# Linear attention and an ELU feed-forward on one core: mm1 in units of two chunks, state decay on GpSimd, two chunks transposed by DMA, one load on a second queue, in a new order of work

## The chip, the cores and the metric

One core of one Trainium2 chip. The metric is the device time of one execution in microseconds (us), the median of several. All runs quoted here are in the fast state with a granted TensorE clock of 0.99 to 1.00. "Span" is the profiled part of an execution; in most runs the time is 1.7 to 1.9 us above it, in a few up to 2.8 (the profiled run of split: 223.31 against 220.5).

## The reference

Two steps. A chunked linear attention with one decay factor per head, then a two-layer feed-forward with ELU between:

```python
# q, k, v: (4, 8, 768, 64); lam: (8,); w_in: (512, 2048); w_out: (2048, 512); all float32
for b in range(nb):                                   # blocks of the sequence
    intra = (qb @ kb^T) * Dmask ; intra = intra @ vb  # Dmask: lam ** (i - j), causal
    inter = (qb * lam_pow) @ kv_state
    out   = intra + inter
    kv_state = lam_block * kv_state + (kb * rev_pow)^T @ vb
x = attention as (3072, 512)
h = x @ w_in
g = where(h > 0, h, exp(min(h, 0)) - 1)               # ELU
return g @ w_out
```

(Shortened; einsums written as products.)

## The kernel before

The kernel works in 24 chunks of 128 rows (4 batches of 6), in a hand-written order of tokens. For a chunk g: `T` transposes q and k, `S` makes the scores psS, `E` masks them into pp, `P` makes the attention output psO and copies it into xt, `U` updates the state. `1:g:j` is one mm1 unit: 16 matmuls of xt with `w_in` into a psH bank (one of two), then e = exp on ScalarE, relu on ScalarE in place, and later g = min(e - 1, relu) on VectorE, which frees the bank. `2:g:j` is one mm2 unit: 4 matmuls of g with `w_out` into psM. Each engine executes its own instructions in the order in which they are written. The parts that the change touches:

```python
GPE = 10                       # chunks below GPE are transposed by PE, the others by DMA
POOL_ORDER = ("iota q1 k1 v1 v0 i1 i0 k2 q2 v2 o0 o1 i3 i2 q3 i5 k3 o2 d0 o3 i4 v3 ...")
OPEN = ("... P4 U4 2:3:2 1:4:0 P5 U2 1:4:1 V3 2:3:3 T6 U5 1:4:2 2:4:0 1:4:3 T7 2:4:1 U3 "
        "1:5:0 1:5:1 2:4:2 S6:7 1:5:2 2:5:0 2:4:3 P6 1:5:3 E7 T8 T9 ... S8:9 2:6:0 E9")
LAGU, LAG_END = 3, 4           # mm2 follows mm1 at 3 units, 4 at the end
# [...]
def att_U(g):
    # [4 matmuls into pu]
    for hh in range(2):
        r = slice(hh * 64, (hh + 1) * 64)
        # [first chunk of a batch: copy]
        (nc.gpsimd if g >= GPE else nc.vector).tensor_tensor(      # stt: decay of the old state
            out=tmp[r], in0=old[r, :, r],
            in1=upp[r].unsqueeze(2).broadcast_to([64, NHP, 64]), op=ALU.mult)
        nc.vector.tensor_tensor(out=new[r, :, r], in0=tmp[r], in1=pu[r, :, r], op=ALU.add)  # st
# [...]
def mm1(g, j):
    flush()                                                        # emits the g that is pending
    # [...]
    pH = ps.tile([128, FB, 128], FP32, tag="psH", bufs=2, name=f"psH{g}_{j}")
    for f in range(FB):
        i, w = wi_of[j * FB + f]
        for kk in range(NHP):
            nc.tensor.matmul(
                pH[:, f, :], lhsT=wi16[i][:, kk, w * 128 : (w + 1) * 128],
                rhs=xt[g][:, kk, :], start=(kk == 0), stop=(kk == NHP - 1))
    e = msb.tile([128, FB, 128], FP32, tag="e", bufs=3, name=f"e{g}_{j}")
    nc.scalar.activation(e[:], pH[:], AF.Exp)
    nc.scalar.activation(pH[:], pH[:], AF.Relu)
    pending.append(((g, j), e, pH))
```

`POOL_ORDER` is the order on GpSimd: loads of q, k, v, of `w_in` blocks (i) and `w_out` blocks (o), and d, the product kd of k with its decay.

Of the kernel before, what the change touches and what calls it, by code (L numbers as in the profile page):

```python
# [7 lines left out]
FP32 = mybir.dt.float32  # L8
# [7 lines left out]
def kernel(  # L16
# [20 lines left out]
    NG = B * NCB  # L37
    FB = 4
    NJ = NFT // FB
    GPE = 10  # L40
    WI = [2] * 8
    WO = [2] * 8
    POOL_ORDER = (
        "iota q1 k1 v1 v0 i1 i0 k2 q2 v2 o0 o1 i3 i2 q3 i5 k3 o2 d0 o3 i4 v3 o5 o4 d2 o7 i6 d3 "
        "d1 i7 o6 q4 k4 v4 q6 d4 k8 k6 v6 d5 d6 k10 q8 d7 q10 v8 v10"
    )
    RAW = "q0 k0"
    FIRST = "q0:0 c0 k0:1 c1 c2"
    OPEN = (
        "V0 Z1 z1 V1 z0 v3:1 Z0 z3 z2 T0 T1 S0 S1 P0 P1 1:0:0 T2 1:1:0 S2 2:0:0 Z2 P2 1:2:0 "  # L50
        "1:0:1 2:1:0 1:1:1 U0 T3 2:2:0 1:2:1 S3 2:0:1 2:1:1 1:0:2 1:1:2 P3 2:2:1 1:2:2 2:1:2 "
        "1:3:0 Z3 U1 2:0:2 1:3:1 1:0:3 2:2:2 1:1:3 2:0:3 1:2:3 T5 2:1:3 1:3:3 T4 2:2:3 1:3:2 "
        "S4:5 2:3:0 E5 2:3:1 P4 U4 2:3:2 1:4:0 P5 U2 1:4:1 V3 2:3:3 T6 U5 1:4:2 2:4:0 1:4:3 T7 "
        "2:4:1 U3 1:5:0 1:5:1 2:4:2 S6:7 1:5:2 2:5:0 2:4:3 P6 1:5:3 E7 T8 T9 1:6:2 V2 P7 U6 "
        "2:5:1 U7 1:6:0 2:5:2 2:5:3 1:6:1 S8:9 2:6:0 E9"
    )
    LAGU, LAG_END = 3, 4
    AT = {"W": -13, "T": -9, "S": -8, "P": -5, "U": -3}
    TAGS = {
        "S0": "M0 M1", "S1": "C D", "S2": "A B", "S3": "A B",  # L60
# [13 lines left out]
    ps = ctx.enter_context(tc.tile_pool(name="ps", bufs=1, space=bass.MemoryType.PSUM))  # L74

    lam_b = cpool.tile([128, H], FP32, name="lam_b")
    nc.scalar.dma_start(out=lam_b[:], in_=lam.unsqueeze(0).broadcast_to([128, H]))
    nc.scalar.preload_act_table_set("natural_log_exp_and_others")



# [12 lines left out]
    def emit_load(w, g0):  # L94
        n = size_of[g0]
        c, b = divmod(g0, B)
        x = {"q": q, "k": k, "v": v}[w]
        src = x[b : b + n, :, c * L : (c + 1) * L].rearrange("b h p d -> p (b h) d")
        if w == "v":
            t = vz1[g0] if n == 1 else vz2[(g0 - 4) // 2 % PB]  # L100
            vg[g0] = t
            dst = t[:, :, 0::2, :]
        else:
            t = asb.tile([128, n, H, 64], FP16, tag=f"{w}n{n}", name=f"{w}n{g0}", bufs=4)
            (qg if w == "q" else kg)[g0] = t
            dst = t[:]
        nc.gpsimd.dma_start(out=dst.rearrange("p b h d -> p (b h) d"), in_=src)  # L107
# [3 lines left out]
    for w in RAW.split():  # L111
        x = {"q": q, "k": k}[w[0]]
        g0 = int(w[1:])
        raw[w] = asb.tile([128, H, 64], FP32, name=f"raw_{w}", tag=f"raw_{w}")
        nc.sync.dma_start(out=raw[w][:], in_=x[g0, :, 0:L].rearrange("h p d -> p h d"))

    def cast_raw(g, w, eng):
        n = f"{w}{g}"
# [40 lines left out]
        nc.gpsimd.iota(iota_c[:], pattern=[[0, 1]], base=0, channel_multiplier=1)  # L159
        nc.gpsimd.iota(iota_r[:], pattern=[[1, 128]], base=0, channel_multiplier=0)  # L160

    kds, qkT, Pt, psS, psO, xt = {}, {}, {}, {}, {}, {}

    def att_kd(g):
        if g // B == NCB - 1:
# [11 lines left out]
    def emit_pool():  # L177
        w = pool_list.pop(0)
        if w == "iota":
            emit_iota()  # L180
        elif w[0] in "qkv":
            emit_load(w[0], int(w[1:]))
        else:
            {"i": emit_wi, "o": emit_wo, "d": att_kd}[w[0]](int(w[1:]))

    while pool_list and pool_list[0][0] != "d":
        emit_pool()

    def zero_v1(i, eng=0):
# [124 lines left out]
    def att_P(g):  # L314
        cb, b = divmod(g, B)
        vt = of(vg, g)
        qt, _ = qkT[g]
        po = bank(f"P{g}", 0, [128, NHP, 128], FP32, f"psO{g}")
        for hp in range(NHP):
            for hh in range(2):  # L320
                b0 = 4 * hp + hh
                nc.tensor.matmul(  # L322
                    po[:, hp, :], lhsT=vt[:, b0 : b0 + 2, :], rhs=Pt[(g, hh)][:, hp, :],
                    start=(hh == 0), stop=(hh == 1 and cb == 0), skip_group_check=True,
                )
            if cb > 0:
                nc.tensor.matmul(  # L327
                    po[:, hp, :], lhsT=st[b][cb % 2][:, hp, :], rhs=qt[:, hp, :],
                    start=False, stop=True, skip_group_check=True,
                )  # L330
        xt[g] = asb.tile([128, NHP, 128], FP16, tag="xt", name=f"xt{g}", bufs=6)
        if g < GPE:
            nc.scalar.copy(out=xt[g][:], in_=po[:])  # L333
        else:
            nc.vector.tensor_tensor(out=xt[g][:], in0=po[:], in1=qs[:], op=ALU.mult)  # L335

    def att_U(g):
        cb, b = divmod(g, B)
        if cb == NCB - 1:
            return  # L340
        vt = of(vg, g)
        pu = bank(f"U{g}", 0, [128, NHP, 128], FP32, f"psU{g}")
        for hp in range(NHP):
            nc.tensor.matmul(  # L344
                pu[:, hp, :].rearrange("p (h e) -> p h e", h=2),
                lhsT=kds[g][:, 2 * hp : 2 * hp + 2, :],
                rhs=vt[:, 4 * hp : 4 * hp + 3 : 2, :], start=True, stop=True,
            )
        new, old = st[b][(cb + 1) % 2], st[b][cb % 2]
        for hh in range(2):  # L350
            r = slice(hh * 64, (hh + 1) * 64)
            if cb == 0:
                nc.vector.tensor_copy(new[r, :, r], pu[r, :, r])
            else:
                tmp = asb.tile([128, NHP, 64], FP32, tag="stt", name=f"stt{g}_{hh}", bufs=4)
                (nc.gpsimd if g >= GPE else nc.vector).tensor_tensor(  # L356
                    out=tmp[r], in0=old[r, :, r],
                    in1=upp[r].unsqueeze(2).broadcast_to([64, NHP, 64]), op=ALU.mult,
                )
                nc.vector.tensor_tensor(  # L360
                    out=new[r, :, r], in0=tmp[r], in1=pu[r, :, r], op=ALU.add
                )


    gts, psM, stores, pending = {}, {}, [], []
# [5 lines left out]

    def flush():
        while pending:
            u, e, r = pending.pop(0)
            g = msb.tile([128, FB, 128], FP16, tag="g", bufs=24, name=f"g{u[0]}_{u[1]}")
            nc.vector.scalar_tensor_tensor(  # L376
                out=g[:], in0=e[:], scalar=-1.0, in1=r[:], op0=ALU.add, op1=ALU.min
            )
            gts[u] = g

    def mm1(g, j):
        flush()
        emit_stores(1)
        pH = ps.tile([128, FB, 128], FP32, tag="psH", bufs=2, name=f"psH{g}_{j}")
        for f in range(FB):
            i, w = wi_of[j * FB + f]
            for kk in range(NHP):
                nc.tensor.matmul(  # L388
                    pH[:, f, :], lhsT=wi16[i][:, kk, w * 128 : (w + 1) * 128],
                    rhs=xt[g][:, kk, :], start=(kk == 0), stop=(kk == NHP - 1),  # L390
                )
        e = msb.tile([128, FB, 128], FP32, tag="e", bufs=3, name=f"e{g}_{j}")
        nc.scalar.activation(e[:], pH[:], AF.Exp)  # L393
        nc.scalar.activation(pH[:], pH[:], AF.Relu)  # L394
        pending.append(((g, j), e, pH))

    mm2_done = {g: 0 for g in range(NG)}

    def mm2(g, j, last=False):
# [6 lines left out]
        for hi, cols in enumerate(halves):  # L406
            for f in range(FB):
                i, w = wo_of[j * FB + f]
                nc.tensor.matmul(  # L409
                    psM[g][:, cols], lhsT=gts[(g, j)][:, f, :], rhs=wo16[i][:, w, cols],  # L410
                    start=first and f == 0, stop=end and f == FB - 1, skip_group_check=True,
                )
            if end:
                out_of(g, cols, nc.vector if last and hi == 0 else nc.scalar)
# [18 lines left out]
    def pool_work(g):  # L433
        if group_of[g][1] == 0 and g + 4 < NG:
            for w in "qkv":
                emit_load(w, g + 4)
        att_kd(g)
        if g >= GPE:
            att_T_dma(g)

# [1 line left out]

    def ready(t):

        if t[0] in "12":
            return
        g = int(t[1:].split(":")[0])
        if t[0] == "P":
# [9 lines left out]
    def run(t):  # L458
# [10 lines left out]
        else:  # L469
            {"T": att_T_pe, "E": att_E, "P": att_P, "U": att_U, "1": mm1, "2": mm2,  # L470
             "V": zero_v, "Z": zero_st, "v": zero_v1, "z": zero_st1,
             "q": lambda g, e: cast_raw(g, "q", e), "k": lambda g, e: cast_raw(g, "k", e),
             "c": lambda i: (emit_qs, emit_mask, emit_ks)[i](), "W": pool_work, "O": emit_stores}[t[0]](*a)

    for t in FIRST.split():
        run(t)
    while pool_list:
        emit_pool()

    prog = OPEN.split()  # L480
    done = set(prog)
    m1 = [(g, j) for g in range(NG) for j in range(NJ) if f"1:{g}:{j}" not in done]
    m2 = [(g, j) for g in range(NG) for j in range(NJ) if f"2:{g}:{j}" not in done]
    extra = {}
    for g in range(0, NG, 2):
        u = 4 * g
        for t, p in (
            (f"W{g}", AT["W"]), (f"W{g + 1}", AT["W"] + 2),
            (f"T{g}", AT["T"]), (f"T{g + 1}", AT["T"] + 1),
# [7 lines left out]
            if t in done or f"{t[0]}{h}" in done or t[0] == "E" and f"S{h}" in done:  # L497
                continue
            extra.setdefault(u + p, []).append(t)
    first = 4 * NG - len(m1)  # L500
    for p in sorted(extra):
        if p < first:
            prog += extra.pop(p)
    n2 = 4 * NG - len(m2)
    for x, (g, j) in enumerate(m1):
        u = first + x
        prog.append(f"1:{g}:{j}")
        prog += extra.pop(u, [])
        lag = LAG_END if u >= 4 * NG - 8 else LAGU
        n = 0  # L510
        while m2 and n2 <= u - lag and n < 2:
            prog.append("2:%d:%d" % m2.pop(0))
            n2 += 1
            n += 1
    for g, j in m2:
        prog.append(f"2:{g}:{j}")
    prog[-1] += ":1"
# [33 lines left out]
```

## Time and profile before

| | before |
|---|---|
| time | 222.81 us median of 4 (222.52 to 223.24) |
| span of the profiled run | 221.4 us |
| PE matmuls | 2548 |
| bare matmul time (worked out below) | 198.8 us |
| PE without matmul issue | 22.6 us |

One more view is needed later: the groups on VectorE by shape from 48 to 87 us, with busy time, mean ns and then the idle time just before the group.

```profile
L376 DVE SCALAR_TENSOR_TENSOR g<-e,psH 128x512 f16<-128x512 f32 x17 | 11.6, 685 | 2.9 <-ACT psH L394 2.1 <-PE psS L300 0.5
L356 DVE TENSOR_TENSOR stt<-st,upp 64x256 f32<-64x256 f16 x12 | 8.0, 666 | 0.1
```

In these 39 us VectorE has 2.9 us of slack ahead of its 17 g, and the decays stt take 8.0 us of it. A g that comes late is one that PE waits for.

For PE I also use a sum of my own over the trace's matmul starts: each matmul is given its undisturbed step (55.6 ns for 128 columns, 108.9 for 256, 215.7 for 512, 34.5 for psS), and what a start is later than that is a gap. "Gap" means this everywhere below. Such a gap includes the drain of a wait, so it is larger than the "idle before" that the profile prints.

### The profile page before, as it was taken

Reading aid. Unit: us, or ns where it says so; the run is one execution under the profiler, and the core shown is the slowest. Engines: PE = TensorE matmul, PEld = TensorE weight load, DVE = VectorE, ACT = ScalarE, POOL = GpSimd, SP = SyncE. Lnnn points to the kernel's source line nnn. Section 1 sums busy time; section 2 is a strip of 40 time slices with the busy share of each in tenths; the row PEclk is TensorE's granted clock in tenths of the full one; section 3 lists DMA queues with packets and bytes.
Section 4 is the critical chain, followed back from the end, with each engine's and each line's share of the span. In section 5 each row is a group of like instructions: output and inputs, shape, how many; then the busy total and the mean of one; then the engine's idle time right before and its main releaser. Section 6 shows DMA issues by size and latency. Waiting matters only on the chain.

```text
span 221.4 us, 6086 instructions
## 1 busy us (share of the span) xinstructions
PE 207.1 (94%) x2548; PEld 156.3 (71%) x2548; DVE 138.6 (63%) x238; ACT 134.8 (61%) x255; POOL 88.6 (40%) x102
## 2 busy tenths in 40 slices
PE   0598999999999999999999999999999999999993
PEld 0486677768768776787787787787787777777761
DVE  5744745489978978666666666656657646634330
ACT  5745657766768566636636636646646645656760
POOL 8996990829972809508508508122000000000000
PEclk9999999999999999999999999999999999999999
DMA  7999999999999999968998998803304401101102
GB/s 114 169 182 186 195 200 167 139 169 120 166 140 181 127 164 135 141 84 93 143 100 100 132 108 95 144 0 98 94 3 98 96 3 47 52 1 50 47 3 95
DMA packets 99804, 24.26 MB, mean 110 GB/s; under 512 B 90432, under 2 KB 96832, under 8 KB 99776
## 3 DMA queue, kind: packets, MB, share of 16 engines
q0 software_dynamic: 78720, 13.37, 83.8%
q1 hardware_dynamic: 20912, 10.49, 22.3%
q8 instruction: 20, 0.33, 0.6%
q14 instruction: 8, 0.07, 0.1%
q10 hardware_dynamic: 144, 0.00, 0.0%
HBM read 27.27 MB, written 6.29 MB: 152 GB/s over the span
## 4 chain that ended last, share of the span: by engine, by line
PE 79%; DVE 11%; ACT 5%; DMA 2%; issue 1%; SPq 0%; DVEq 0%; ACTq 0%
PE psH L388 34%; PE psM L409 33%; PE psO L322 5%; DVE g L376 3%; PE psS L300 3%; DVE stt L356 2%; DMA raw_k<-in_k_dram 2%; PE psO L327 2%; DVE pp L309 2%; PE psU L344 2%; DVE qT L288 1%; DVE st L360 1%; ACT e L393 1%; ACT psH L394 1%; PE psT L281 1%
## 5 line engine op out<-in xcount | busy, mean ns | idle before, releaser
L388 PEld LDWEIGHTS <-wi 128*128 128x128 f16 x1536 | 94.0, 98 | 22.0 <-issue 2.2
L388 PE MATMUL psH<-xt,wi 128*128 128x128 f16 x1536 | 102.2, 220 | 1.8 <-ACT xt L333 0.7
L393 ACT ACTIVATE e<-psH 128x512 f32<-128x512 f32 x96 | 57.3, 597 | 68.3 <-PE psH L388 68.0
L409 PE MATMUL psM<-wo,g 128*128 128x512 f16 (+1 forms) x388 | 97.6, 377 | 0.8 <-DVE osb L422 0.5
L376 DVE SCALAR_TENSOR_TENSOR g<-e,psH 128x512 f16<-128x512 f32 x96 | 65.6, 684 | 44.1 <-ACT psH L394 42.8
L394 ACT ACTIVATE psH<-psH 128x512 f32<-128x512 f32 x96 | 56.9, 593 | 0.0
L409 PEld LDWEIGHTS <-g 128*128 128x128 f16 x388 | 33.7, 98 | 26.8 <-issue 0.7
L309 DVE TENSOR_TENSOR pp<-psS,mask 128x512 f16<-128x512 f32 x48 | 30.7, 682 | 5.1 <-PE psS L300 5.1
L107 POOL DMA_DIRECT2D vz<-in_v_dram x14 | 15.1, 1085 | 38.5 <-PE psU L344 38.0
L169 POOL TENSOR_TENSOR kd<-kn,ks 128x512 f16<-128x512 f16 x20 | 21.3, 1073 | 11.2 <-DMA kn<-in_k_dram 10.6
L322 PE MATMUL psO<-pp,vz 128*128 128x128 f16 x192 | 19.1, 226 | 1.2 <-DVE pp L309 1.2
L360 DVE TENSOR_TENSOR st<-stt,psU 64x256 f16<-64x256 f32 x32 | 13.4, 419 | 7.3 <-PE psU L344 6.3
L335 DVE TENSOR_TENSOR xt<-psO,qs 128x512 f16<-128x512 f32 x14 | 9.7, 691 | 11.9 <-PE psO L327 11.9
L322 PEld LDWEIGHTS <-vz 128*128 128x128 f16 x192 | 15.1, 101 | 2.5 <-issue 1.8
L424 ACT COPY osb<-psM 128x512 f32<-128x512 f32 (+1 forms) x24 | 13.9, 579 | 4.5 <-PE psM L409 4.5
L356 POOL TENSOR_TENSOR stt<-st,upp 64x256 f32<-64x256 f16 x20 | 12.2, 608 | 10.3 <-DVE st L360 9.5
L107 POOL DMA_DIRECT2D qn<-in_q_dram x13 | 14.8, 1142 | 0.5 <-DMA wi<-in_moe_w_in_dram 0.3
L327 PE MATMUL psO<-qT,st 128*128 128x128 f16 x80 | 14.4, 219 | 0.0
L107 POOL DMA_DIRECT2D kn<-in_k_dram x13 | 14.4, 1107 | 0.0
L288 DVE TENSOR_TENSOR qT<-psT,qs 128x512 f16<-128x512 f16 x10 | 6.6, 681 | 5.2 <-PE psT L281 5.2
L281 PE MATMUL psT<-ident,qn 128*128 128x128 f16 x40 | 4.6, 247 | 5.4 <-DVE qn L122 5.4
L333 ACT CAST xt<-psO 128x512 f16<-128x512 f32 x10 | 5.9, 588 | 6.0 <-PE psO L322 4.0
(41 smaller groups left out, 90.2 us busy)
## 6 DMA issues: line engine op xcount, KB each, us to landing
out_dram<-osb SPq DMA_DIRECT2D x23, 256.0 KB, 3.4
qn<-in_q_dram POOLq DMA_DIRECT2D x10, 256.0 KB, 7.6
kn<-in_k_dram POOLq DMA_DIRECT2D x10, 256.0 KB, 7.4
vz<-in_v_dram POOLq DMA_DIRECT2D x10, 256.0 KB, 8.2
wi<-in_moe_w_in_dram POOLq DMA_DIRECT2D x8, 256.0 KB, 8.3
wo<-in_moe_w_out_dram POOLq DMA_DIRECT2D x8, 256.0 KB, 8.8
vz<-in_v_dram POOLq DMA_DIRECT2D x4, 128.0 KB, 5.9
qn<-in_q_dram POOLq DMA_DIRECT2D x3, 128.0 KB, 6.4
```

What stands on the lines that cost most here:

```text
L107: nc.gpsimd.dma_start(out=dst.rearrange("p b h d -> p (b h) d"), in_=src)
L169: nc.gpsimd.tensor_tensor(out=kd[:], in0=of(kg, g), in1=ks[:].unsqueeze(2).broadcast_to([128, H, 64]), op=ALU.mult,)
L309: nc.vector.tensor_tensor(out=P[:], in0=pts[hh][:], in1=mask[:, hh::2, :], op=ALU.mult)
L322: nc.tensor.matmul(po[:, hp, :], lhsT=vt[:, b0 : b0 + 2, :], rhs=Pt[(g, hh)][:, hp, :], start=(hh == 0), stop=(hh == 1 and cb == 0), skip_ ...
L327: nc.tensor.matmul(po[:, hp, :], lhsT=st[b][cb % 2][:, hp, :], rhs=qt[:, hp, :], start=False, stop=True, skip_group_check=True,)
L356: (nc.gpsimd if g >= GPE else nc.vector).tensor_tensor(out=tmp[r], in0=old[r, :, r], in1=upp[r].unsqueeze(2).broadcast_to([64, NHP, 64]), ...
L360: nc.vector.tensor_tensor(out=new[r, :, r], in0=tmp[r], in1=pu[r, :, r], op=ALU.add)
L376: nc.vector.scalar_tensor_tensor(out=g[:], in0=e[:], scalar=-1.0, in1=r[:], op0=ALU.add, op1=ALU.min)
L388: nc.tensor.matmul(pH[:, f, :], lhsT=wi16[i][:, kk, w * 128 : (w + 1) * 128], rhs=xt[g][:, kk, :], start=(kk == 0), stop=(kk == NHP - 1),)
L393: nc.scalar.activation(e[:], pH[:], AF.Exp)
L394: nc.scalar.activation(pH[:], pH[:], AF.Relu)
L409: nc.tensor.matmul(psM[g][:, cols], lhsT=gts[(g, j)][:, f, :], rhs=wo16[i][:, w, cols], start=first and f == 0, stop=end and f == FB - 1, ...
```

## The change

Intent: fewer PE instructions (mm1 of 256 columns, from chunk 4 on, and no PE transposes for chunks 8 and 9), VectorE relieved of 12 decays, a denser opening.

```diff
-    GPE = 10
+    GPE = 8
+    GSIZE = {**{g: 1 for g in range(4)}, **{g: 2 for g in range(4, NG, 2)}}
     POOL_ORDER = (
-        "iota q1 k1 v1 v0 i1 i0 k2 q2 v2 o0 o1 i3 i2 q3 i5 k3 o2 d0 o3 i4 v3 o5 o4 d2 o7 i6 d3 "
+        "k2 v1 q2 iota q1 k1 i1 v0 i0 o1 v2 i3 o0 i2 q3 o2 k3 d0 d2 i4 d1 i5 o3 o7 v3 o5 o4 d3 "
+        "i6 i7 o6 k4 q4 k10 k6 d4 v4 v8 q6 d5 q10 m4 v10 m5 m6 v6 d6 k8 q8 d7 m7"
 [...]
     OPEN = (
+        [...] "S4:5 2:3:0 1:3:3 P4 E5 V3 2:3:1 U4 2:3:2 P5 U5 1:4:1 2:3:3 U3 M 1:4:0 W8 M W9 T6 "
+        "1:4:2 T7 1:4:7 V2 S6:7 1:4:3 2:4:0 1:4:4 E7 2:4:1 1:4:5 P6 1:4:6 U7 P7 U6 2:4:2 1:6:0 "
+        "1:6:1 2:4:3 S8:9 1:6:2 2:5:2 1:6:4 W10 2:5:1 W11 2:5:3 E9 1:6:3 2:6:0 2:5:0 U8 P8 "
+        "1:6:5 1:6:6 2:6:1 P9 U9 1:6:7 2:6:2"
-    LAGU, LAG_END = 3, 4
+    LAGU = 7
 [...]
-        nc.sync.dma_start(out=raw[w][:], in_=x[g0, :, 0:L].rearrange("h p d -> p h d"))
+        (nc.sync if w[0] == "q" else nc.scalar).dma_start(
+            out=raw[w][:], in_=x[g0, :, 0:L].rearrange("h p d -> p h d"))
 [...]
+    def att_M(g):                       # token m / M / W: the decay, written ahead of its update
+        # [...]
+        for hh in range(2):
+            r = slice(hh * 64, (hh + 1) * 64)
+            tmp = asb.tile([128, NHP, 64], FP32, tag="stt", name=f"stt{g}_{hh}", bufs=8)
+            nc.gpsimd.tensor_tensor(
+                out=tmp[r], in0=old[r, :, r],
+                in1=upp[r].unsqueeze(2).broadcast_to([64, NHP, 64]), op=ALU.mult)
+            stt[(g, hh)] = tmp
 [...]
-    def mm1(g, j):
+    def mm1(g0, j):                     # g0: first chunk of a group of n = 1 or 2
 [...]
-        for f in range(FB):
+        for f in range(FB // n):
+            i, w = wi_of[j * (FB // n) + f]
             for kk in range(NHP):
                 nc.tensor.matmul(
-                    pH[:, f, :], lhsT=wi16[i][:, kk, w * 128 : (w + 1) * 128],
-                    rhs=xt[g][:, kk, :], start=(kk == 0), stop=(kk == NHP - 1),
+                    pH[:, f * n * 128 : (f + 1) * n * 128],
+                    lhsT=wi16[i][:, kk, w * 128 : (w + 1) * 128],
+                    rhs=xg[g0][:, kk, :], start=(kk == 0), stop=(kk == NHP - 1),
 [...]
-        lag = LAG_END if u >= 4 * NG - 8 else LAGU
-        n = 0
-        while m2 and n2 <= u - lag and n < 2:
+        n = 2
+        while m2 and need[m2[0]] <= u - 2 and n and len(m2) - (len(m1) - 1 - x) > LAGU:
```

Cut: the whole of `OPEN`, the tiles of two chunks, the moved activation-table load, the load of `lam` on SyncE, assertions.

## The prediction

> **What bounds the kernel now.** First the page's engine totals and slices, to see which engine is full and when.
>
> ```profile
> PE 207.1 (94%) x2548; PEld 156.3 (71%) x2548; DVE 138.6 (63%) x238; ACT 134.8 (61%) x255; POOL 88.6 (40%) x102
> ...
> PE   0598999999999999999999999999999999999993
> ...
> DVE  5744745489978978666666666656657646634330
> ...
> POOL 8996990829972809508508508122000000000000
> ...
> DMA  7999999999999999968998998803304401101102
> ```
>
> The tensor engine (PE) is full from slice 3 to the end; VectorE (DVE) comes near full only in slices 9 to 16, about 50 to 90 us; the DMA engines are full for the first 90 us. A busy PE may still be waiting inside a modelled latency, so next comes the chain of waits in order of time, which shows issue time. First a steady stretch, then one inside the DVE-heavy part.
>
> ```profile
> 103.43 0.55 PE psS L300 x16
> 103.98 0.97 PE psM L409 x4
> 104.95 0.89 PE psH L388 x16
> 105.84 0.86 PE psM L409 x4
> 106.71 0.89 PE psH L388 x16
> ```
>
> ```profile
> 71.48 0.78 DVE stt L356
> 72.26 0.03 issue
> 72.28 0.02 DVEq L360
> 72.30 0.04 issue
> 72.35 0.41 DVE st L360
> 72.76 0.01 issue
> 72.78 0.67 DVE stt L356
> 73.44 0.02 issue
> 73.47 0.03 DVE st L360
> 73.50 0.42 issue
> 73.92 0.70 DVE g L376
> ```
>
> In the first, one PE group follows another with no gap: 16 mm1 matmuls of 128 columns take 0.89 us (55.6 ns each), 4 mm2 matmuls of 512 columns take 0.863 us (215.7 ns each). The chain is pure PE from 87 to about 199 us: a pair of chunks needs 8x0.89 + 8x0.863 + 0.66 (psS) + 1.33 (psO) + 0.44 (psU) = 16.45 us, and the pattern repeats every 16.5 us. In the second, the chain runs through DVE's state decay (stt), the state update and the ELU combine g, while PE waits for g.
>
> Adding up all matmuls at these paces: mm1 96x0.89 = 85.4, mm2 96x0.863 = 82.8, psS 12x0.66 = 7.9, psO 15.1, psU 4.45, transposes 20x0.222 = 4.45; together 200.2 us. The profiled span is 221.4, so 21.2 us are loss. Where: the same sum taken for stretches of the windows view gives 11.0 lost before 13.3 us (the loads and the setup), 3.3 from 13.3 to 26.9, 0.7 to 40.6, about 1.9 from 48 to 87, nothing worth naming to 186, and 3.5 around the last matmuls and the final copy and store. Split where chunk 4's psO begins (48.3 us), 15.1 lie before and 6.1 after. The time per run is 1.6 above the span.
>
> **The Trainium skill and this trace.** (1) "TensorE: Matmul & The Clock Gate", section "Back-to-back issue gap", gives N/2.4 + 2.5 ns for a warm isolated matmul, and about 81 ns (N=128) and 131 ns (N=512) for a real stream of weight loads and matmuls. This trace follows the first formula (55.6 and 215.7 ns) and contradicts the second pair. (2) "GPSIMD Engine Reference", section 1 (Specifications), says the SBUF interface is shared with VectorE, with contention for DVE instructions with two SBUF inputs. The decay stt is such an instruction (state and upp both in SBUF). The trace agrees: alone it takes 407 ns, and up to 1279 ns; this is the slow one, beside GpSimd's kd:
>
> ```profile
> 49.39 1.03 POOL L169 TENSOR_TENSOR kd<-kn,ks 128x512 f16<-128x512 f16 x1 [4.10 <-DMA kn<-in_k_dram]
> 49.42 1.28 DVE L356 TENSOR_TENSOR stt<-st,upp 64x256 f32<-64x256 f16 x1
> ```
>
> (3) "DMA: Bandwidth & Descriptors", section "Issuing engines are not separate DMA queues": DMAs from several engines share the same 16 engines, so a second queue only saves issue time. So moving raw_k to ScalarE's queue can save at most the 0.5 us between the two SyncE issues (0.74 and 1.25 us).
>
> **The change, part by part.**
>
> *mm1 in pairs.* Chunks 4 to 23 go from 1280 matmuls of 128 columns to 640 of 256; the columns stay. From 55.6 and 215.7 ns a column costs 0.417 ns and an instruction 2.2 ns; so 640 instructions fewer save 1.4 us. Elementwise work is unchanged (96 exp, relu and g of 512 columns), as is mm2. An mm1 unit still fills one of two psH buffers, now in 0.873 us. The mm2 lag rises to 7 units and stays there to the end, which should remove the two bubbles around 200 us (0.3 us).
>
> *Chunks 8 and 9 by DMA.* 16 PE transposes leave: 16x55.6 ns = 0.89 us of the bound engine. DVE loses two qT (0.68 each) and gains two scaled xt copies (0.69): nothing. ScalarE loses four copies of 0.59, off the path. SyncE gets four transposes of about 1.3 us issue.
>
> *Decay on GpSimd.* 12 stt, 8.0 us, leave DVE; 12x0.61 = 7.3 us come to GpSimd, placed before the updates need them. DVE is 78 to 95% busy from 50 to 90 us and these are on the chain with 2.4% of the span, 5.3 us. But PE's loss there is only 1.9 us, because matmuls were queued meanwhile; no more than that can be won.
>
> *The head.* iota moves behind three loads on GpSimd, so (1.06+0.88+0.88 us of issue) it ends near 4.1 us instead of 1.15. Then row, ident and causT (0.96 us), and loglam_p after them: qs on ScalarE starts near 5.5 instead of 4.42, and the cast of raw_k near 6.7 instead of 6.08, although raw_k now lands near 5. I expect the first transposes 0.6 us later and the first mm1 near 14.0 (13.36 before): a loss, if the later opening does not hide it.
>
> *The new opening.* After the first mm1 the new order puts mm1 of chunks 0 and 1 earlier. What limits it is data: loads land about one 256 KB weight block per 1.25 us, some 8 to 10 us after issue. The landing view has for the block issued at 17.5 us:
>
> ```profile
> wi<-in_moe_w_in_dram POOLq DMA_DIRECT2D x1, 256.0 KB, 10.0
> ```
>
> Counting blocks in the new order at that rate (starting 0.5 us earlier, as iota no longer precedes the first load), wi 4 and 5 land near 25.7 us. PE reaches the unit that needs them (chunk 0, third quarter) near 25, so it starts near 26. From there nothing in the list of landings is late (o5/o4 near 31.4 against 32.9 needed, i7 near 34 against 35.7, q4 near 37.7 against 39.4), so PE runs dense: 20.2 us of work to chunk 4's psO at 46.2 us. Before, it began at 48.3 with 0.64 us more work done. Loss before this point 13.6 instead of 15.1: gain 1.5.
>
> *From there to the end of the written-out order.* I went through it by hand with the trace's durations (e 0.60, relu 0.50 after it, g 0.69, pp 0.65 each in pairs, copies 0.59). Bare work 33.8 us; waits I find: 0.45 for chunk 5's xt copy (a two-chunk unit needs both chunks' copies), 0.5 for a psH buffer around chunk 7's transpose, 0.3 to 0.7 for kT7 and a g. Some 1.65 in all. With the end bubbles gone the loss after chunk 4's psO, apart from the unchanged tail of 3.3, falls from 2.8 to 1.65: gain 1.1.
>
> Sum: 1.4 + 0.9 + 1.5 + 1.1 = 4.9 us; 222.96 - 4.9 = 218.1. I shade it to 217.8, because the order looks searched for on the chip, so that some of the small waits I found by hand may not be there.
>
> **Rivals.** *A: only the PE work goes.* The opening remains bound by the loads (DMA slices of 9) and the DVE gaps become other gaps: then 1.4 + 0.9 = 2.3 us and 220.6. For it: DMA share is full to 85 us and the bytes are the same. Against: DVE is the releaser on the chain three times between 52 and 86 us, and its load falls by 8 of 40 us. *B: the opening loses nothing more.* If DVE's relief and the order remove nearly all waits from 13 us on, PE needs 197.9 of work + 11 head + 3.3 tail + 1 = 213.2 of span, 214.8. Against: the weight blocks cannot land earlier, and waiting for wi 4 and 5 alone costs about 1. *C: a new wait.* GpSimd is in order: decays wait for DVE's updates and hold up loads and kd behind them; chunk 4's v is now issued behind a kd that waits for k to land (near 37, landing near 44 to 46 against a need at 46.2), and the transposes of chunks 8 and 9 need q and k that land near 60, plus 4x1.3 us of issue, against a need at 66.6. Each may cost 1 to 2 us: 219 to 221. *D: the late iota costs its 0.6 us fully:* 218.4.
>
> **Range and chances.** Between A and B the centre is 217.8; 8 in 10 I give to 215.4 to 220.0. Two per cent faster is 218.5, 0.7 above my centre with a spread of about 1.8: chance 0.65. Within 2%: 0.34. Slower by 2% would need a new wait of 9 us: 0.01.
>
> **What would show it.** Right: psH matmuls of 256 columns at about 109 ns in the chain and a steady period near 16.35 us; no DVE stt, and GpSimd stt x32 of 0.61 us; psT x64; iota near 4 us and the cast of kn near 6.7; the third quarter of chunk 0 starting near 26, chunk 4's psO near 46 and chunk 8's first mm1 near 82. Wrong: a 256-column matmul well over 109 ns; a long PE wait on a DMA of vz, kn or wi; a wait for kT or qT of chunks 8 or 9 by DMA; GpSimd stt in the list of what DVE's st waits for. If chunk 4's psO is no earlier than 48, rival A holds.

## The result, and the profile after

| | before | after |
|---|---|---|
| time, median | 222.81 us (222.52 to 223.24, 4 runs) | 221.07 us (220.66 to 221.41, 4 runs) |
| span, profiled | 221.4 us | 219.3 us |
| PE matmuls | 2548 | 1892 |
| bare matmul time | 198.8 us | 196.4 us |
| PE gaps, start to psO of chunk 4 | 15.4 us (to 48.25) | 14.4 us (to 46.58) |
| PE gaps, from there to the last matmul | 3.9 us | 5.0 us |
| from the start of the last matmul to the end | 3.3 us | 3.6 us |

The ratio is 0.992 (95% interval 0.9895 to 0.9944): faster by 0.8%, which counts as the same at 2%. A ratio is the mean time of one kernel's fast runs over that of the other's of the same rounds, so it is not quite the ratio of the medians. The predicted time was 217.8, and 221.07 lies outside the range of 215.4 to 220.0.

The table already holds the answer in outline. The matmul work fell by 2.4 us, the opening lost 1.1 us less, and what follows the opening lost 1.1 us *more*, where the prediction had counted on 1.1 less. The gaps as a whole did not change: 19.3 us in both kernels.

The page's totals and slices after:

```profile
PE 203.7 (93%) x1892; PEld 144.0 (66%) x1892; DVE 130.6 (60%) x226; ACT 132.5 (60%) x251; POOL 95.5 (44%) x114
...
PE   0398999999999998999999999999999999999993
...
DVE  3775447585885578557557567567567547434410
...
DMA  5999999999996999979919919114118110110021
```

656 instructions are gone from PE (640 from mm1 and 16 transposes). VectorE's row no longer shows a run of 8 and 9 in slices 9 to 16. The DMA row is as full up to slice 16 as before. PE's slice 1 fell from 5 to 3: the start is later.

The groups that answer the ones of before: first two from the page, then VectorE's g in the stretch from 46.5 to 86.7 us, in which no stt is left on VectorE.

```profile
L427 PE MATMUL psH<-xt,wi 128*128 128x256 f16 (+1 forms) x896 | 99.6, 258 | 2.5 <-DVE g L410 1.9
...
L364 POOL TENSOR_TENSOR stt<-st,upp 64x256 f32<-64x256 f16 x32 | 19.5, 610 | 1.4
```

```profile
L410 DVE SCALAR_TENSOR_TENSOR g<-e,psH 128x512 f16<-128x512 f32 x19 | 13.0, 685 | 10.2 <-ACT psH L434 9.8 <-PE psS L310 0.4
```

VectorE's slack before g rose from 2.9 to 10.2 us, as intended; and yet the mm1 group has 2.5 us of idle time ahead of it, 1.9 of it put down to g. The relief arrived, but waits for g remain. The chain in time order, a steady stretch:

```profile
99.11 0.55 PE psS L310 x16
99.67 0.97 PE psM L449 x4
100.64 0.87 PE psH L427 x8
...
115.45 0.55 PE psS L310 x16
```

The period is 115.45 - 99.11 = 16.34 us (16.50 before; the prediction expected 16.35). The same view, at places where it leaves PE:

```profile
19.03 7.20 DMA wi<-in_moe_w_in_dram
26.27 0.62 PE psH L427 x8
...
50.07 0.59 ACT xt L349
50.70 1.05 PE psH L427 x8
...
64.36 4.67 DMA kT<-kn
69.47 0.98 PE psH L427 x8
...
82.64 0.87 PE psH L427 x8
83.92 0.57 issue
85.09 0.69 DVE g L410
85.82 1.05 PE psH L427 x8
```

Four kinds of wait. At 26.27 PE waits for a weight block, as predicted ("near 26"), but only for a gap of 0.24 us, where the prediction had reckoned with about 1. At 50.70 a two-chunk unit waits for the copy of its second chunk. At 69 the scores of chunk 9 wait for kT by DMA. At 85.82 an mm1 unit waits for a psH bank. VectorE's timeline shows why the last one happens:

```profile
83.88 1.29 DVE L319 TENSOR_TENSOR pp<-psS,mask 128x512 f16<-128x512 f32 x2 [0.20 <-PE psS L310]
85.09 0.68 DVE L410 SCALAR_TENSOR_TENSOR g<-e,psH 128x512 f16<-128x512 f32 x1
85.68 1.28 DVE L319 TENSOR_TENSOR pp<-psS,mask 128x512 f16<-128x512 f32 x2
```

PE had issued mm1 at 82.48, psS, and mm1 at 84.00, and wants a third bank from 84.9 on, with only two there. The first is freed by the g at 85.09, so at about 85.8. The relu ahead of that g ended near 84.7 on ScalarE, so the two pp cost some 0.4 us; the other 0.5 is the way through e, relu and g itself, some 2 us, longer than the units that PE had to do meanwhile. One mm2 unit (0.86 us) more between the two mm1 units would cover nearly all of it.

The same kind of wait stands once more in the opening, where the new order puts three mm1 units after each other with no mm2 between:

```profile
18.70 1.07 PE L427 MATMUL psH<-xt,wi 128*128 128x128 f16 x16 [0.80 <-DVE g L410]
```

It is a gap of 0.96 us. The g that frees the bank starts at 17.95 on VectorE, behind two state copies, though its relu ended at 17.39. best2 shows below what removing this wait is worth.

All gaps over 0.15 us after psO of chunk 4, without the 0.11 us that follows every psS and without the 0.68 us at the last copy, which both kernels have (my sum):

```
before:  0.25 and 0.31 (58.7, 59.9)  0.25 (74.7)  0.61 (85.9)  0.36 (201.7)                  sum 1.8
after:   0.61 (50.7, copy of chunk 5)  0.50 (55.8, psH bank, g behind qT)
         0.33 (57.3, kT of chunk 7)    0.19 (66.6)
         0.42 (69.1, kT of chunk 9 by DMA)    0.93 (85.8, psH bank, g behind pp)             sum 3.0
```

### The profile page after: what moved, and what is told of

Same layout as the page of the kernel before. It is cut to its first block, busy times and chain, and to the rows that moved or that the text cites. A ratio compares the mean times of both kernels' runs of the same rounds, so it can differ in the third digit from the quotient of the medians.

```text
span 219.3 us, 4793 instructions
## 1 busy us (share of the span) xinstructions
PE 203.7 (93%) x1892; PEld 144.0 (66%) x1892; DVE 130.6 (60%) x226; ACT 132.5 (60%) x251; POOL 95.5 (44%) x114
## 4 chain that ended last, share of the span: by engine, by line
PE 80%; POOL 8%; DMA 5%; ACT 2%; issue 2%; DVE 1%; SPq 0%; POOLq 0%; DVEq 0%; ACTq 0%
PE psM L449 36%; PE psH L427 34%; PE psO L332 4%; DMA wi<-in_moe_w_in_dram 3%; PE psS L310 2%; DMA kT<-kn 2%; PE psO L337 2%; POOL wi L149 2%; PE psU L381 2%; POOL kd L175 1%; POOL kn L110 1%; POOL vz L110 1%; POOL qn L110 1%; POOL wo L156 1%; ACT e L433 1%
## 5 line engine op out<-in xcount | busy, mean ns | idle before, releaser
L427 PE MATMUL psH<-xt,wi 128*128 128x256 f16 (+1 forms) x896 | 99.6, 258 | 2.5 <-DVE g L410 1.9
L427 PEld LDWEIGHTS <-wi 128*128 128x128 f16 x896 | 77.0, 98 | 27.5 <-DVE g L410 3.2
L449 PEld LDWEIGHTS <-g 128*128 128x128 f16 x388 | 35.7, 98 | 27.6 <-issue 0.7
L110 POOL DMA_DIRECT2D vz<-in_v_dram x14 | 15.4, 1100 | 24.4 <-PE psU L381 24.4
L364 POOL TENSOR_TENSOR stt<-st,upp 64x256 f32<-64x256 f16 x32 | 19.5, 610 | 1.4
L332 PE MATMUL psO<-pp,vz 128*128 128x128 f16 x192 | 18.6, 223 | 0.0
L351 DVE TENSOR_TENSOR xt<-psO,qs 128x512 f16<-128x512 f32 x16 | 11.1, 691 | 11.7 <-PE psO L337 11.7
L332 PEld LDWEIGHTS <-vz 128*128 128x128 f16 x192 | 15.2, 100 | 1.6 <-issue 0.4
L337 PE MATMUL psO<-qT,st 128*128 128x128 f16 x80 | 14.4, 219 | 0.0
L291 PE MATMUL psT<-ident,qn 128*128 128x128 f16 x32 | 3.8, 253 | 8.6 <-DVE qn L128 7.2
L310 PE MATMUL psS<-qT,kT 64*128 64x128 f16 x192 | 8.8, 229 | 0.4 <-DMA kT<-kn 0.2
L291 PEld LDWEIGHTS <-qn 128*128 128x128 f16 x32 | 2.5, 110 | 9.4 <-DVE qn L128 7.2
```

Source lines behind the costliest of these rows:

```text
L110: nc.gpsimd.dma_start(out=dst.rearrange("p b h d -> p (b h) d"), in_=src)
L332: nc.tensor.matmul(po[:, hp, :], lhsT=vt[:, b0 : b0 + 2, :], rhs=Pt[(g, hh)][:, hp, :], start=(hh == 0), stop=(hh == 1 and cb == 0), skip_ ...
L337: nc.tensor.matmul(po[:, hp, :], lhsT=st[b][cb % 2][:, hp, :], rhs=qt[:, hp, :], start=False, stop=True, skip_group_check=True,)
L364: nc.gpsimd.tensor_tensor(out=tmp[r], in0=old[r, :, r], in1=upp[r].unsqueeze(2).broadcast_to([64, NHP, 64]), op=ALU.mult,)
L427: nc.tensor.matmul(pH[:, f * n * 128 : (f + 1) * n * 128], lhsT=wi16[i][:, kk, w * 128 : (w + 1) * 128], rhs=xg[g0][:, kk, :], start=(kk = ...
L449: nc.tensor.matmul(psM[g][:, cols], lhsT=gts[(g, j * FB + f)], rhs=wo16[i][:, w, cols], start=first and f == 0, stop=end and f == FB - 1, ...
```

## The experiments

All have five rounds beside the kernel before, whose median was 222.77 to 222.90; all were correct. A difference in time is worked out as the difference of ratios times 222.8. "Span" is that of the profiled run.

**Theory.** The parts do what the prediction said, one by one; what is missing went into waits that the new order makes itself, above all through the mm2 lag. **Rival 1:** the decays were worth nothing, since PE's loss was not VectorE's doing. **Rival 2:** the late head or the loads took the gain.

### split: two-chunk units, but 128-column matmuls

```diff
-            for kk in range(NHP):
-                nc.tensor.matmul(pH[:, f * n * 128 : (f + 1) * n * 128], [...] rhs=xg[g0][:, kk, :], [...])
+            for c in range(n):
+                for kk in range(NHP):
+                    nc.tensor.matmul(
+                        pH[:, (f * n + c) * 128 : (f * n + c + 1) * 128], [...]
+                        rhs=xg[g0][:, kk, c * 128 : (c + 1) * 128], [...])
```

> The changed kernel with one thing undone: every two-chunk unit still fills one psH buffer from two chunks, in the same order, but with 128-column matmuls (1280 instead of 640). Theory (what the change won is PE work alone, 1.4 us of it from fewer mm1 instructions, 2.2 ns each): span 219.3 + 1.4 = 220.7, steady period from 16.35 back to 16.48 us, time about 222.4, ratio to before near 0.998. Rival (the pairing saves nothing on PE and the gain lies in the new order): span unchanged at 219.3.

Measured: 222.23 us, ratio 0.9974 (0.995 to 0.9998), span 220.5, so 1.2 us of both time and span more than the change, and the steady period is 16.50 again. The 640 instructions are worth about 1.2 us, close to the 1.4 that the prediction worked out from the two matmul durations. It follows that this part is right.

### decay_dve: the decays of chunks 4 to 9 back on VectorE, at the update

```diff
-        if cb == NCB - 1:
+        if cb == NCB - 1 or g < 10:
             return
 [...]                                   # in att_U:
+                if g < 10:
+                    tmp = [...]
+                    nc.vector.tensor_tensor(out=tmp[r], in0=old[r, :, r], in1=upp[...], op=ALU.mult)
```

> The changed kernel with the decays of chunks 4 to 9 back on VectorE, right at the state update, as before; the rest unchanged. My prediction's reasoning (VectorE's relief removes PE waits between 48 and 87 us): PE's gap loss between chunk 4's psO and chunk 8's first mm1 rises from 2.3 to 4 us or more, span 221 or more. Rival theory (in the new order these waits come from psH buffers, the second chunk's xt copy and the transposes by DMA, not from the decays; so moving the decays was worth little): span 219.3 to 219.9.

Measured: 223.97 us, ratio 1.0056 (1.003 to 1.0082), span 222.3: 3.0 us more than the change. PE's timeline has one new wait of 2.05 us as a gap:

```profile
69.01 1.05 PE L435 MATMUL psH<-xt,wi 128*128 128x256 f16 x8 [1.88 <-DVE g L418]
```

Further gaps of 0.64 and 0.50 us follow at 86 to 87 us. Rival 1 falls: in the new order the decays matter more than the prediction had allowed ("no more than that can be won", 1.9). The other side of it: with 2.4 us less matmul work but without this part, the new order would be *slower* than the kernel before (222.3 against 221.4). So the order itself costs something.

### before_decay: the kernel before, with only the decays moved

```diff
-        [...] d1 i7 o6 q4 k4 v4 q6 d4 k8 k6 v6 d5 d6 k10 q8 d7 q10 v8 v10
+        [...] d1 i7 o6 q4 k4 v4 q6 d4 k8 k6 v6 d5 m4 m5 d6 k10 q8 d7 q10 v8 v10 m6 m7
-        [...] 1:3:0 Z3 U1 2:0:2 [...] 2:4:1 U3 1:5:0 [...]
+        [...] 1:3:0 Z3 U1 M M 2:0:2 [...] 2:4:1 U3 M M 1:5:0 [...]
```

(with `att_M` from the change; units, loads, transposes and mm2 lag as before)

> The kernel before, with this one part of the change added: the decays of chunks 4 to 9 on GpSimd ahead of need; its order, one-chunk units and everything else kept. Theory (the relief of VectorE does remove PE waits in the old order, as the prediction had it, and it is the new two-chunk order that spends that gain on waits of its own): PE's gap loss between 48 and 87 us falls from 1.8 to 0.8 or less, span 220.2 to 220.6 against 221.4. Rival (these waits were not worth anything in the old order: others take their place, or GpSimd, now with 7.3 us more in its queue, delays loads): span 221.2 or more.

Measured: 221.63 us, ratio 0.9946 (0.9932 to 0.996), span 219.8. That is 1.2 us less time (1.6 of span), and of the five gaps between 48 and 202 us only the one of 0.36 us near 200 is left. VectorE's g from 48 to 86.5 us:

```profile
L403 DVE SCALAR_TENSOR_TENSOR g<-e,psH 128x512 f16<-128x512 f32 x17 | 11.7, 686 | 6.2 <-ACT psH L421 6.1
```

The slack before g is 6.2 us in place of 2.9. This run is the one that accounts for the change: the decays alone, in the old order, give 1.2 to 1.6 us, and the matmul work 2.4, together 3.6 to 4.0 if the parts simply add. The change as a whole gave 1.8 (2.1 of span). So about 1.8 us net was lost to the new order. The gaps say where: against before_decay the change has 1.0 us less of them up to psO of chunk 4 (14.4 against 15.3), but 2.5 more from there on (5.0 against 2.4), and 0.25 more tail.

### lag5: mm2 lag of 5 everywhere

```diff
-    LAGU = 7
+    LAGU = 5
```

> The changed kernel with the mm2 lag of 5 units in place of 7. Theory: with 7, after the written-out order two mm1 units of chunks 8 and 9 follow each other without an mm2 between them, and PE waits 0.93 us at 85.8 us for a psH buffer; with 5 an mm2 stands between them and the wait goes: span 218.3 to 218.6. Rival (the wait only moves to a later psH buffer, because the g operations come late whatever PE does): span 219.1 to 219.4.

Measured: 221.1 us, ratio 0.9925 (0.9903 to 0.9948), span 219.0: no difference in time. The gap of 0.93 at 85.8 us is gone, and so is the one of 0.42 for kT of chunk 9; but 0.38 comes at 196.6 and 0.83 at 210.9 us, where mm2 runs out of finished g near the end. So the lag of 7 has a purpose, and its price is paid once, at 85.8 us. The next run takes each where it is good.

### lag57: lag 5 at the start of the generated order, 7 afterwards

```diff
-  while m2 and need[m2[0]] <= u - 2 and n and len(m2) - (len(m1) - 1 - x) > LAGU:
+  while m2 and need[m2[0]] <= u - 2 and n and len(m2) - (len(m1) - 1 - x) > LAGU - (u < 43) - (u < 44):
```

> The changed kernel with an mm2 lag of 5 units up to chunk 12 and 7 after, the two steps up taken where chunk 12's and 13's psO matmuls stand between mm1 units. With 5 throughout, the wait of 0.93 us at 85.8 went but 0.38 and 0.83 came back at 197 and 211 us. Theory: both gone, span 218.2 to 218.5. Rival (waits of this kind only move): 219 or more.

Measured: 219.88 us, ratio 0.9866 (0.9846 to 0.9886), span 217.9: 1.2 us less time than the change, 1.4 of span. PE's timeline where the wait was, in the change and then in lag57:

```profile
84.00 1.05 PE L427 MATMUL psH<-xt,wi 128*128 128x256 f16 x8
85.82 1.05 PE L427 MATMUL psH<-xt,wi 128*128 128x256 f16 x8 [0.77 <-DVE g L410]
```

```profile
83.55 1.05 PE L427 MATMUL psH<-xt,wi 128*128 128x256 f16 x8
84.44 1.89 PE L449 MATMUL psM<-wo,g 128*128 128x512 f16 x8
86.16 1.04 PE L427 MATMUL psH<-xt,wi 128*128 128x256 f16 x8
```

Two mm2 units now lie ahead of the mm1 unit, and nothing waits. The work is only reordered: the mm2 units that come earlier here would otherwise come later, with PE full either way. Of the 1.4 us, 0.93 is the gap aimed at. The other 0.42 is the kT wait, which this profile does not have; since the profiles of lag5 and iota hardly have it either, while those of the change and of head do (0.42, 0.45), it depends on when the DMAs happen to land, and I do not put it down to the lag. This is the largest single item of what was missing.

### pe_t89: chunks 8 and 9 transposed by PE again

```diff
-    GPE = 8
+    GPE = 10
-        [...] U7 P7 U6 2:4:2 1:6:0 [...]
+        [...] U7 P7 U6 2:4:2 T8 T9 1:6:0 [...]
```

> The changed kernel with chunks 8 and 9 transposed on PE again (and their scaling by VectorE moved back from xt to qT). It puts 16 matmuls, 0.89 us, back on PE, and takes away the wait of chunk 9's scores for kT by DMA (0.42 us at 69 us). Theory: span 219.3 + 0.5, 219.6 to 220.0. Rival (PE has idle time there to hide them): span 219.3 or less. Second rival (VectorE's qT in front of other work costs more): 220.2 or more.

Measured: 221.69 us, ratio 0.9951 (0.9937 to 0.9966), span 220.4: 0.7 us more time than the change, 1.1 of span. The time is the better measure here: 220.4 is the longest span of its six runs (median 219.9), and 0.46 us of it are opening gaps, above all a late k of chunk 3 (0.70 at 24.07), which the edit does not touch. The 0.89 us of transposes return, and the tail is 0.24 us shorter (more on this at the end). The 0.42 for kT goes, and this comes in its place (0.43 as a gap), with 0.28 at 70.7:

```profile
66.42 0.38 PE L291 MATMUL psT<-ident,qn 128*128 128x128 f16 x4 [0.27 <-DVE st L392]
```

So the DMA transposes are worth about 0.7 us, the wait and the longer tail that they bring included; the prediction's 0.89 stands for the work on PE, and its rival C (1 to 2 us lost to late kT) has at most the 0.42.

### iota and head: the start

```diff
 iota:
-        "k2 v1 q2 iota q1 k1 i1 v0 i0 [...]
+        "iota k2 v1 q2 q1 k1 i1 v0 i0 [...]
 head:
-        "k2 v1 q2 iota q1 k1 i1 v0 i0 [...]
+        "iota q1 k1 k2 v1 q2 i1 v0 i0 [...]
```

> The changed kernel with iota first again on GpSimd, ahead of the loads. The late iota delays the first PE work to 7.24 us (5.43 before). Theory (the opening is gated at 26.3 us by the load of wi block 5, which GpSimd issues at 19.0 us in its queue, so the head is hidden): first transposes 1 to 1.8 us earlier, but the third quarter of chunk 0 still starts near 25.5 to 26.5, span 219.0 to 219.6. Rival (the head adds fully): span 217.6 to 218.2.

Measured for iota: 220.66 us, ratio 0.9916 (0.9886 to 0.9946), span 218.7. Within its interval nothing is gained (the median is 0.4 us lower, but one of the six runs took 222.5). The profile of it has no kT wait of 0.42 to speak of, which alone makes 0.3 of the 0.6 us of span; another 0.24 is the opening, in which PE no longer waits for block 5 (psO of chunk 4 at 46.34, 46.58 in the change).

> The changed kernel with iota, then q and k of chunk 1 as the first loads (k, v, q of chunks 2, 1, 2 after them). With iota alone first, the second transposes still waited for q of chunk 1 until 9.28 us. Theory (the first mm1 follows the second chunk's transposes): second transposes at 7.3 to 8.0 and first mm1 1 us earlier than 15.2, but wi block 5 still lands near 26, so the span falls by less, to 218.3 to 218.9. Rival: no limit by wi block 5, span 217.5 or less.

Measured for head: 221.01 us, ratio 0.9917 (0.9902 to 0.9933), span 219.2. No gain; the 218.3 to 218.9 of its theory were missed. PE's timeline in head:

```profile
7.01 0.61 PE L291 MATMUL psT<-ident,qn 128*128 128x128 f16 x4 [7.01 <-DVE qn L128]
...
12.53 1.04 PE L332 MATMUL psO<-pp,vz 128*128 128x128 f16 x8 [0.81 <-DMA vz<-in_v_dram]
```

The first transposes start at 7.01 us against 7.24 in the change, with iota out of the way: what they wait for is the cast of q of chunk 0, and its load lands only 5.0 to 5.5 us after its issue in these orders, where it took 4.2 in the kernel before (rawk_sync shows why). With q and k of chunk 1 loaded earlier, v of chunk 0 or 1 comes later and the wait moves to it. The third mm1 unit starts at 19.12 us, no earlier than in the change (18.70), behind the same wait for a psH bank. Further on stands the landing of block 5: 26.23 us in the change, 25.98 in head and iota, which PE then meets almost without a gap. So an earlier head is worth at most 0.24 us at this point.

### rawk_sync: k of chunk 0 back on the first queue

```diff
-        (nc.sync if w[0] == "q" else nc.scalar).dma_start(
+        nc.sync.dma_start(
```

> The changed kernel with k of chunk 0 back on SyncE's queue behind lam and q. Theory (the cast of k waits for qs on ScalarE, which waits for the late iota, so k's landing is covered; and the opening is hidden behind wi block 5): k lands about 0.5 us later, the cast starts at 6.9 to 7.4, span 219.1 to 219.6. Rival (the second queue is worth its half microsecond or more): 219.8 or more.

Measured: 221.03 us, ratio 0.9916 (0.9899 to 0.9934), span 219.2. The second queue is worth nothing: its k was not what the head waits for. It even did harm that the time does not show. The load of q is issued at 1.20 us in both kernels; with k behind it on the same queue it lands at 5.03, with k issued at 0.73 on the second queue at 6.67. In rawk_sync the first transposes start at 6.50 in place of 7.24; what then holds the cast of q until 5.77 is VectorE's mask work, which waits for the late iota.

### best1: lag57 with the copy of chunk 5 covered

```diff
-        [...] U4 2:3:2 P5 U5 1:4:1 2:3:3 U3 M 1:4:0 W8 [...]
+        [...] U4 P5 2:3:2 U5 1:4:1 U3 M 1:4:0 2:3:3 W8 [...]
```

(and the edit of lag57)

> Lag 5 then 7 as in lag57, and two mm2 moved in the written-out order: one behind chunk 5's psO, so that its xt copy on ScalarE is covered (0.61 us of PE wait at 50.7), one behind the second mm1 unit of chunks 4 and 5, so that a psH buffer is free in time (0.50 us at 55.8). Theory (waits that the two-chunk order made, each removable by work that is at hand): span 217.9 less 0.8 to 1.1, 216.8 to 217.1. Rival (they move to the next psH wait): 217.6 or more.

Measured: 219.58 us median, ratio 0.9883 (0.9846 to 0.992), span 217.3, between what theory (216.8 to 217.1) and rival (217.6 or more) expected. Two of its six runs are long (220.99 and 221.97), so the mean, and with it the ratio, is no better than that of lag57; the profiled span is 0.6 shorter. The gaps of 0.61 at 50.7 and 0.50 at 55.8 are gone: the mm2 unit lies between P5 and the unit that needs its copy. But the wait for kT of chunk 7 grew from 0.33 to 1.03. The trace shows that the waits were linked; how much of the 0.6 lasts over many runs is not settled by this run alone.

### best2: best1 with the loads reordered

```diff
-        "k2 v1 q2 iota q1 k1 i1 v0 i0 [...] k3 d0 d2 i4 d1 i5 o3 o7 [...]
+        "iota q1 k1 v0 k2 q2 v1 i1 i0 [...] k3 d0 i4 i5 d2 o3 d1 o7 [...]
-        [...] 1:0:0 P2 U0 1:1:0 1:2:0 [...]
+        [...] 1:0:0 P2 1:1:0 U0 1:2:0 [...]
```

> best1 with the opening's loads put in order of need: iota, q and k of chunk 1, v of chunk 0, then k, q of chunk 2; wi blocks 4 and 5 ahead of two of GpSimd's kd; chunk 0's state update one mm1 unit later. Theory (the opening is gated twice, by the first chunks' loads and by the place of wi blocks 4 and 5 in GpSimd's queue, so only both together help): third quarter of chunk 0 at 24 to 25, span 1 to 2 us under best1. Rival (DMA bandwidth fixes when the blocks land): within 0.4 of best1.

Measured: 219.47 us (219.11 to 219.73), ratio 0.9844 (0.9828 to 0.9859), span 217.2: faster than the kernel before by 1.6% and the fastest of all. GpSimd's timeline in it shows weight blocks 4 and 5 issued together:

```profile
15.80 1.56 POOL L149 DMA_DIRECT2D wi<-in_moe_w_in_dram  x2
```

Block 5 is issued 2.4 us earlier (16.61 against 19.03 in the change), lands 0.27 us earlier (25.96 against 26.23), and PE waits for it until 26.0 us (26.27 in the change). The rate at which the loads arrive, not the place in GpSimd's order, sets that point. The other edit of best2 also removed the psH wait of 0.96 us at 18.7: the third mm1 unit starts at 17.65. PE then waits 0.77 us at 23.34 for k of chunk 3, and psO of chunk 4 starts at 46.31, 46.37 in best1. A wait ahead of a limit set by the loads was worth nothing. The span is that of best1; what best2 shows is mainly best1's edit without its two long runs, and I do not claim a gain for the load order.

### best3: best1 with T7 directly after T6

```diff
-        [...] W9 T6 1:4:2 T7 1:4:7 V2 [...]
+        [...] W9 T6 T7 1:4:2 1:4:7 V2 [...]
```

> best1 with chunk 7's PE transposes moved ahead of the next mm1 unit, beside chunk 6's. In best1 PE waits 1.03 us at 56.7 for kT of chunk 7, whose copy stands behind an exp and a relu on ScalarE. Theory: the copy goes ahead of them, the wait goes, span 217.3 less 0.5 to 1.0. Rival (the two mm1 units behind them then wait for a psH buffer instead, for ScalarE has the same work to do in that stretch): span within 0.3 of 217.3.

Measured: 220.17 us, ratio 0.9874 (0.9856 to 0.9892), span 218.2: slower than best1 in the span by 0.9 (0.39 of it in the opening, which the edit does not touch) and by 0.6 in the median; both expectations were missed. The wait in best2 (best1 has the same 1.03 us gap), and the one that takes its place in best3:

```profile
56.64 0.40 PE L310 MATMUL psS<-qT,kT 64*128 64x128 f16 x8 [0.85 <-ACT kT L299]
```

```profile
57.89 1.03 PE L427 MATMUL psH<-xt,wi 128*128 128x256 f16 x8 [1.31 <-DVE g L410]
```

With kT earlier on ScalarE, the e and relu behind it are later, and a psH bank is late by 1.49 us in place of 1.03. A wait that stems from the same engine's work moves when the order is changed; it does not go.

## Why the prediction was wrong

By its own steps:

- **mm1 in pairs (1.4 us): right.** 1.2 in split, period 16.34 against 16.35 predicted. The 256-column matmul takes 0.87 / 8 = 109 ns.
- **Chunks 8 and 9 by DMA (0.9): right.** 0.89 of PE work and 0.7 of time in pe_t89. Together these two make the 2.4 us by which the bare matmul time fell.
- **Decay on GpSimd (at most 1.9): right in mechanism.** Alone it gives 1.2 to 1.6 us in the old order. In the new order its absence costs 3.0; it is worth what the rest of the order leaves it.
- **The head (0.6 later): wrong, without effect.** The first transposes came at 7.24, not near 6.0, and the first mm1 at 15.2, not 14.0. The effect of iota was estimated well (qs at 5.70, the cast of k at 6.88; 5.5 and 6.7 predicted). What was left out is the load of q of chunk 0: the prediction let the second queue save at most 0.5 us, and did not ask what it costs the load beside it. q landed at 6.67 instead of 4.93, and with k back on its queue at 5.03 (rawk_sync). "A loss, if the later opening does not hide it": it hides nearly all of it.
- **The opening (1.5): right in mechanism, 0.4 too high.** Block 5 came at 26.27 ("near 26"), psO of chunk 4 at 46.58 (46.2 predicted). Measured gain 1.1. The wait for block 5 was 0.24 us and not about 1, because PE had lost 0.96 us at 18.7 that the prediction did not foresee; best2 shows that the loads set the end of the opening all the same.
- **"From there to the end of the written-out order [...] the loss [...] falls from 2.8 to 1.65: gain 1.1": the step that failed.** It came out as 1.1 more gaps, and the tail 0.25 longer. Two terms were wrong. The 2.8 of before was too high: about 0.7 of it is the gap at the last copy, which belongs to the unchanged tail; the waits that the trace shows there come to 1.8 (the prediction's own stretches give 1.9 + 3.5 = 5.4 after chunk 4's psO, not the 6.1 that it split off). And the 1.65 of after stopped too soon. The waits that it found are there, close in size (0.45, 0.5 and 0.3 to 0.7 expected; 0.61, 0.50, and 0.33 with 0.19 measured, 1.63 in sum). But the hand trace ended at chunk 8's first mm1 (82 predicted, 82.48 measured), and the 0.93 at 85.8 lies two units behind it, at the seam between the written-out order and the generated one. lag57 shows that wait to be the work of the mm2 lag of 7. The remaining 0.42 is kT of chunk 9, which the prediction had named as a rival and not booked.
- **The shading from 218.1 to 217.8** rested on the order being searched for on the chip. lag57 found a better one with a single edit, so it was no ground for shading.

Rival A ("only the PE work goes", 220.6) is close in the number and wrong in its reason: the opening did gain, and VectorE's waits did go; the order's own waits took the same amount back. What would have told it in advance: the prediction looked at psH banks only around chunk 7's transpose, and booked the lag of 7 as a gain at the end alone, without asking which mm2 units it takes away at the start.

The longer tail belongs to the DMA transposes of chunks 8 and 9: it is 3.54 to 3.63 us in every kernel that has them, and 3.3 before and in pe_t89, which has the new order without them. The last store lands 2.40 us after the start of the last matmul either way; by SyncE's records in the traces, one semaphore wait then remains before the kernel's end in the kernel before and in pe_t89, and five in the change, some 0.06 us each. Why they stand in that order is not shown.

What stays open: whether best1 itself is more variable; and the waits around chunk 7, which best3 only moved.

## What to carry to other kernels

When the bound engine runs in order and shares double buffers with others, count for each reordering which unit it puts next to which: a run of producers longer than the buffers, with no consumer between, waited for a buffer (0.96 us at 18.7, 0.93 at 85.8) although the other engine had slack on average. Trace the new order by hand beyond the last written token, to the point where the repeating pattern has turned over once, since the seam is where the lag rule first acts. Test a change of several parts one by one on the old kernel as well (before_decay), because a part's worth differs between the two orders.

## What the Trainium skill lacked or had wrong

- "TensorE: Matmul & The Clock Gate", section "Back-to-back issue gap": its figures for a sustained stream, 81 ns (N=128) and 131 ns (N=512), are not what these runs show; 55.6, 109 and 215.7 ns for 128, 256 and 512 columns are, which is its formula for the isolated case, in a stream of weight loads and matmuls.
- "GPSIMD Engine Reference", section 4.1 (Engine selection), calls a two-input elementwise operation about twice as slow there as on VectorE. The decay takes 610 ns on GpSimd (32 of them) and 407 ns alone on VectorE, a ratio of 1.5. (Beside GpSimd's work one took 1279 ns on VectorE.)
- "DMA: Bandwidth & Descriptors", section "DMA Transpose (X-bar)", gives no time to landing. In the change the 16 kT of 128x512 took 2.5 to 8.0 us (median 3.9) from issue, beside 1.2 to 1.3 us of issue for most, and the four issued between 55 and 75 us 4.7 to 8.0 (median 5.6); the scores of chunk 9 waited for it by 0.42 us.
- No page that bears on this says what a psH bank costs in an in-order kernel: it comes free some 2 us after its matmuls end (e 0.60, relu 0.50 behind it, g 0.69, and their latencies), and some 0.4 us later where two pp stood ahead of the g.
